# Shifted V copied by two engines, and one batch's keys transposed a stage earlier, in an attention + gated FFN kernel

## The chip, the cores and the metric

The kernel runs on one core of a Trainium2 chip. A core has five engines that run side by side and wait for one another by semaphores: TensorE (PE in the profile, with its weight loads as PEld), VectorE (DVE), ScalarE (ACT), GpSimd (POOL) and SyncE (SP), which here only issues DMA transfers. Each engine works through its own list of instructions in order. The metric is the device time of one execution in microseconds, lower is better.

## The reference

Eight batches of 576 tokens, 8 heads of 64. Attention looks 32 tokens to each side, and 8 global tokens see, and are seen by, everything. Its output goes through a gated feed-forward layer with a gated residual:

```python
scores = scale * np.matmul(q, k.transpose(0, 1, 3, 2))
mask = np.abs(pos[:, None] - pos[None, :]) <= window          # window = 32
mask = mask | is_global[:, None] | is_global[None, :]
scores = np.where(mask, scores, -1000000000.0)
attn = exp(scores - max); attn /= sum(attn); x = np.matmul(attn, v)                 # to [4608, 512]
g = x @ w_gate                                                 # 512 -> 1536
gelu = 0.5 * g * (1.0 + erf(g * inv_sqrt2))
ffn_out = gelu * (x @ w_val) @ w_out                           # 1536 -> 512
out = x + sigmoid(x @ w_res) * ffn_out
```

Inputs and output are float32; the products inside run in bfloat16.

## The kernel before

**Tiling.** The 4608 tokens are cut into 9 chunks of 512. A chunk has 8 windows of 64 queries; a batch has 9 windows, so chunk 1 holds window 8 of batch 0 and windows 0 to 6 of batch 1. A window of 64 queries meets 128 keys. Keys and queries lie transposed in `kt` and `qt`, V lies in rows: `ve` holds blocks of 128 tokens for windows with even i, `vo` the same blocks shifted by 64 tokens for windows with odd i (line 506). `vo` is made from `ve` alone: its lower half of partitions is the upper half of the same block of `ve`, its upper half the lower half of the next block (`shift_v`, lines 102 to 104). All these buffers are in pairs, by the parity of the batch: batch 2 uses the same `kt`, `qt`, `ve`, `vo` as batch 0. `q_st` and `k_st` are single staging buffers, in rows, ahead of the transposing.

**Stages.** The order is written out by hand; a framework adds the semaphore waits. For chunk c, line 702's loop of 12 steps makes the two FFN input products (`g_ps`, `v_ps`, line 550), with ACT's gelu and a DVE product after each. From line 762 follows F(c): for each of four token tiles a gate (`r_ps`, line 568) and three thirds of the output product (`f_ps`, line 593), 16 pieces called `work_f`, between which the attention of chunk c+1 is laid: `scores` (`sc`, exponential on ACT, then the product with the mask on DVE, line 486), `global_rows` (`sn`; its result `vgs` is a DVE product, line 444), `values` (`nd`, from which DVE makes `xtok`), and `turn_x`. A third's end is `prb` on DVE, `ob` on POOL (line 599) and a store issued by SP (line 601). `global_scores(b)` (`sg` and `ss`, lines 415 to 426) for batch b = c+1 is the last thing before F(c) when c > 0; `sg` reads all of `qt`, `ss` all of `kt`. For batch 1 it stands at the start of F(0), and its exponential and the product into `gt` (line 435) follow.

**Loads of batch b >= 2.** `turn_qk(b)` at the start of chunk b-1 (line 696) issues ten DMA transposes on SP, five for q, then five for k. `load_v(b)` on POOL's queue follows (line 697). At step 8 `shift_v(b)` is issued on SP, and `load_qk(b+1)` refills `q_st`, then `k_st`, on POOL's queue, each piece once its transpose has landed.

**Batches 1 and 2 at the start.** They are loaded as float32 and cast by engines. POOL's list in chunk 0, step 5 (lines 720 to 739), is: casts of q and k of batch 1, two casts of `w_res`, five casts of V into `ve[1]`, `shift_v(1)` as two DMAs of POOL's own queue, six casts of `w_out` pieces (14 to 19), three gathers of global rows. The first half of `vo[1]`, as float32, is also where the last V piece of batch 1 is staged. In F(0), lines 772 to 796, batch 2's k and q are loaded (`load_second`), k cast by ACT in one go and q by POOL in three.

Of the kernel before, what the change touches and what calls it, by code (L numbers as in the profile page):

```python
# [23 lines left out]
def kernel(  # L24
# [12 lines left out]
    nc = tc.nc  # L37
# [28 lines left out]
    q_st = const.tile([128, NQT, H * D], BF16, name="q_st", tag="q_st")  # L66
# [35 lines left out]
    def shift_v(b, eng=nc.sync):  # L102
        eng.dma_start(vo[b % 2][0:64, 0:4, :, :], ve[b % 2][64:128, 0:4, :, :])
        eng.dma_start(vo[b % 2][64:128, 0:4, :, :], ve[b % 2][0:64, 1:5, :, :])
# [31 lines left out]
    def cast_piece(n, copy):  # L136
        copy(pieces[n][1], staged(n))
# [56 lines left out]
    def cast_second(what, r0, r1, copy):  # L194
        for r in range(r0, r1):
            n = min(128, S - 128 * r)
            copy({"q": q_st, "k": k_st}[what][0:n, r, :], place2[what][r][0:n, :])
# [208 lines left out]
        copy(dst[:, p, c0:c0 + SM].rearrange("c (s r) -> c s r", r=RPP), ps.rearrange("c r s -> c s r"))  # L406


    def turn_qk(b):
        for src, dst, c0 in ((q_st, qt[b % 2], 0), (k_st, kt[b % 2], 32)):  # L410
            for r in range(NQT):
                n = min(128, S - 128 * r)
                nc.sync.dma_start(dst[:, :, c0 + 128 * r:c0 + 128 * r + n], src[0:n, r, :], transpose=True)

    def global_scores(b):
        sg = psn.tile([128, 2, 512], F32, name="sg", tag="nd")
        for hf in range(2):
            for p in range(NP):
                nc.tensor.matmul(sg[:, hf, 0:288], kgz[b % 2][:, p, :], qt[b % 2][:, p, 288 * hf:288 * hf + 288],  # L419
                                 start=(p == 0), stop=(p == NP - 1))  # L420
        ss = pss.tile([128, 5, 64], F32, name="ss", tag="sc")
        for c in range(5):
            for p in range(NP):
                nc.tensor.matmul(ss[:, c, 16 * p:16 * p + 16], kt[b % 2][:, p, 128 * c:128 * c + 128],
                                 qgz[b % 2][:, p, :], start=True, stop=True)
        return sg, ss

    def global_exp(b, sg, ss):
        rk = 64 * (b % 2)
        rq = 64 - rk  # L430
        nc.scalar.activation(ptg[b % 2][:, :, rq:rq + 64], ss, ACTF.Exp, bias=0.0, scale=SCALE)
        g = gt[b % 2][rk:rk + 64, 64:64 + S]
        nc.scalar.activation(g.rearrange("p (a c) -> p a c", a=2), sg[rk:rk + 64, :, 0:288], ACTF.Exp,
                             bias=0.0, scale=SCALE)
        nc.vector.tensor_tensor(g, g, maskg[rk:rk + 64, :], ALU.mult)
# [89 lines left out]
    def turn_x(c, t):  # L525
        mine = xt[c % 2][:, :, 128 * t:128 * t + 128]
        if c > 1 and t < 3:
            nc.sync.dma_start(mine, xtok[c % 2][:, t, :], transpose=True)
            return
        tx = pss.tile([128, NKT, 128], BF16, name="tx", tag="sc")  # L530
        for kk in range(NKT):
            nc.tensor.transpose(tx[:, kk, :], xtok[c % 2][:, t, 128 * kk:128 * kk + 128], ident)
        (nc.vector.tensor_copy if c or t == 3 else nc.scalar.copy)(mine, tx)  # L533
# [159 lines left out]
    for c in range(NCH):  # L693
        b = c + 1
        if b < B and c:
            turn_qk(b)
            load_v(b)
            if c in (2, 4):
                for what in "kqv":
                    gather(what, c // 2 + 1)  # L700
        held = None
        for j in range(NFF):
            if c or j > 1:
                ffn_in(c, j)
            if c == 0:
                if j == 0:
                    mask_rows(0, NW)
                elif j == 1:
                    mask_rows(NW, NWM)
                    zero_k(1)  # L710
                elif j == 2:
                    zero_gt(1, nc.vector)
                    zero_globals(1)
                    for n in range(1, B // 2):
                        nc.vector.tensor_single_scalar(idx[:, n:n + 1], idx[:, 0:1], float(2 * H * S * n), ALU.add)
                elif j == 3:
                    spread_vg(1, nc.vector)
                elif j == 4:
                    spread_qk(1, compact, 0, {"k": DVE, "q": ACT})
                elif j == 5:  # L720
                    zero_v(1, nc.vector)
                    hot_rows(1)
                    for p in (0, 1, 2, 3, -1):
                        for what in "kq":
                            cast_pair(1, p, what, POOL)
                    load_vraw(1)
                    for n in (14, 15):
                        load_piece(n)
                    for n in (12, 13):
                        cast_piece(n, POOL)  # L730
                    for c5 in range(5):
                        cast_v(1, c5, POOL)
                    shift_v(1, nc.gpsimd)
                    for n in range(16, 20):
                        load_piece(n)
                    for n in range(14, 20):
                        cast_piece(n, POOL)
                    for what in "kqv":
                        gather(what, 1)
                if j > 6:  # L740
                    for what in "kq":
                        turn_pair(1, (0, 1, 2, 3, -1)[j - 7], what)
            elif b < B:
                if c % 2 == 1:
                    n0, n1 = b // 2, b // 2 + 1
                    if j == 8:
                        double_qk(n0, n1)
                    elif j == 9:
                        got = turn_globals(n0, n1)
                        for what in "kq":  # L750
                            DVE(compact[what][:, n0:n1, :], got[what])
                        spread_v(n0, n1)
                if j == 8:
                    shift_v(b)
                    if b + 1 < B:
                        load_qk(b + 1)
                if j == 9:
                    spread_qk(b, compact, (b // 2) * 128, {"k": DVE, "q": DVE})
                    spread_vg(b, nc.vector)
                if j == 11:  # L760
                    held = global_scores(b)
        work_f = [w for t in range(4) for w in ffn_out(c, t)]
        if c == 0:
            global_exp(1, *global_scores(1))
            work_f[0]()
            scores(1, 0)(0, 4)
            work_f[4]()
            work_f[8]()
            mask = scores(1, 1)
            work_f[12]()  # L770
            global_rows(1)
            for what in "kq":
                load_second(what)
            cast_second("k", 0, NQT, ACT)
            work_f[1]()
            values(1, 0)
            mask(0, 2)
            work_f[5]()
            values(1, 1)
            mask(2, 4)  # L780
            work_f[2]()
            turn_x(1, 0)
            work_f[6]()
            values(1, 2)
            turn_x(1, 1)
            work_f[3]()
            cast_second("q", 0, 1, POOL)
            values(1, 3)
            work_f[7]()
            cast_second("q", 1, 3, POOL)  # L790
            turn_x(1, 2)
            work_f[9]()
            work_f[10]()
            turn_x(1, 3)
            work_f[11]()
            cast_second("q", 3, NQT, POOL)
            for n in (13, 14, 15):
                work_f[n]()
            continue
        jobs = {n: [] for n in range(16)}  # L800
        if c + 1 < NCH:
            if held is not None:
                jobs[0].append(lambda: global_exp(b, *held))
                jobs[3].append(lambda: global_rows(b))
            held_mask = {}

            def half(quad):
                held_mask[quad] = scores(c + 1, quad)

            jobs[1] += [lambda: half(0), lambda: held_mask[0](0, 4)]  # L810
            for t in range(4):
                jobs[5 + 2 * t].append(lambda t=t: values(c + 1, t))
                jobs[7 + 2 * t].insert(0, lambda t=t: turn_x(c + 1, t))
            jobs[5].append(lambda: half(1))
            jobs[6].append(lambda: held_mask[1](0, 2))
            jobs[7].append(lambda: held_mask[1](2, 4))
        for n in range(16):
            for w in jobs[n]:
                w()
            work_f[n]()  # L820
# [29 lines left out]
```

## Time and profile before

| | |
|---|---|
| median of 5 runs | 407.12 us (405.8 to 408.34) |
| the profiled execution | 409.42 us, its span 407.7 us |
| TensorE busy | 390.0 us (96%), mean granted clock 0.995 |
| DVE / ACT / POOL busy | 206.0 / 170.9 / 168.5 us |
| SP's DMA queue | 41.88 MB, 45.0% of 16 DMA engines |
| POOL's DMA queue | 10.37 MB, 44.9% of 16 DMA engines |
| HBM read / written | 39.19 / 9.44 MB |

The span runs from the first to the last recorded instruction; the profiled execution's own time is 1.7 us longer. In the profile a row names the engine, the line of the kernel, the operation and `out<-in` by tile names. A bracket gives the idle time of the engine before the row and what ended it. The chain is followed back from the last instruction, at each step to what released it. TensorE's granted clock is given as a share of full speed.

### The profile page before, as it was taken

Reading aid. Unit: us, or ns where it says so; the run is one execution under the profiler, and the core shown is the slowest. Engines: PE = TensorE matmul, PEld = TensorE weight load, DVE = VectorE, ACT = ScalarE, POOL = GpSimd, SP = SyncE. Lnnn points to the kernel's source line nnn. Section 1 sums busy time; section 2 is a strip of 40 time slices with the busy share of each in tenths; the row PEclk is TensorE's granted clock in tenths of the full one; section 3 lists DMA queues with packets and bytes.
Section 4 is the critical chain, followed back from the end, with each engine's and each line's share of the span. In section 5 each row is a group of like instructions: output and inputs, shape, how many; then the busy total and the mean of one; then the engine's idle time right before and its main releaser. Section 6 shows DMA issues by size and latency. Waiting matters only on the chain.

```text
span 407.7 us, 8114 instructions
## 1 busy us (share of the span) xinstructions
PE 390.0 (96%) x3176; PEld 208.5 (51%) x3176; DVE 206.0 (51%) x430; ACT 170.9 (42%) x282; POOL 168.5 (41%) x206
## 2 busy tenths in 40 slices
PE   4899998997999999999999999999999999999995
PEld 2674555443654465446544654456445644554443
DVE  6668656344554554465544553566336534463422
ACT  6664572433523462336323633352435343633320
POOL 8788766746128712562276325521600220021012
PEclk9999999998999999999999999999999999999999
DMA  8999999599929993999399938993992210031002
GB/s 245 255 383 343 232 304 212 145 142 172 91 79 113 188 111 84 95 165 121 84 123 148 136 90 109 164 123 85 87 147 55 79 64 2 0 92 54 1 26 79
DMA packets 152151, 53.30 MB, mean 131 GB/s; under 512 B 136432, under 2 KB 141424, under 8 KB 152112
## 3 DMA queue, kind: packets, MB, share of 16 engines
q1 hardware_dynamic: 76000, 41.88, 45.0%
q0 software_dynamic: 75552, 10.37, 44.9%
q8 instruction: 25, 0.41, 0.5%
q10 hardware_dynamic: 560, 0.52, 0.4%
q14 instruction: 14, 0.11, 0.1%
HBM read 39.19 MB, written 9.44 MB: 119 GB/s over the span
## 4 chain that ended last, share of the span: by engine, by line
PE 81%; DMA 13%; SPq 2%; POOL 2%; issue 1%; DVE 0%; ACTq 0%; DVEq 0%; POOLq 0%
PE f_ps L593 22%; PE g_ps L550 20%; PE v_ps L550 20%; PE r_ps L568 7%; PE nd L508 4%; DMA extra<-in_moe_w_val_dram 3%; DMA vo<-ve 2%; SPq L177 2%; PE sc L464 2%; PE nd L502 2%; DMA kt<-k_st 2%; DMA wo_t<-in_k_dram 2%; PE sn L441 2%; DMA vraw<-in_v_dram 1%; DMA xtok<-in_v_dram 1%; PE sg L419 1%
## 5 line engine op out<-in xcount | busy, mean ns | idle before, releaser
L557 DVE SCALAR_TENSOR_TENSOR ht<-gsb,v_ps 128x512 bf16<-128x512 bf16 x108 | 74.2, 687 | 94.7 <-PE v_ps L550 89.1
L599 POOL TENSOR_TENSOR ob<-prb,xtok 128x512 f32<-128x512 f32 x35 | 40.4, 1153 | 184.5 <-DVE prb L597 182.6
L556 ACT ACTIVATE gsb<-g_ps 128x512 bf16<-128x512 f32 x108 | 64.5, 597 | 122.7 <-PE g_ps L550 120.4
L550 PE MATMUL g_ps<-xt,wg_t 128*128 128x512 bf16 (+1 forms) x440 | 111.2, 375 | 0.4 <-ACT xt L533 0.3
L550 PE MATMUL v_ps<-xt,wv_t 128*128 128x512 bf16 (+1 forms) x440 | 111.2, 375 | 0.0
L593 PE MATMUL f_ps<-wo_t,ht 128*128 128x512 bf16 x420 | 100.4, 379 | 0.0
L550 PEld LDWEIGHTS <-wv_t 128*128 128x128 bf16 x440 | 43.0, 98 | 50.2
L550 PEld LDWEIGHTS <-wg_t 128*128 128x128 bf16 x440 | 42.6, 98 | 49.1 <-issue 0.4
L593 PEld LDWEIGHTS <-ht 128*128 128x128 bf16 x420 | 37.9, 98 | 37.3
L571 ACT ACTIVATE rsb<-r_ps 128x512 bf16<-128x512 f32 x36 | 21.6, 604 | 75.2 <-PE r_ps L568 75.1
L471 ACT ACTIVATE pt<-sc 128x512 bf16<-128x512 f32 x72 | 37.4, 610 | 4.2 <-PE sc L464 4.2
L597 DVE SCALAR_TENSOR_TENSOR prb<-rsb,f_ps 128x512 f32<-128x512 bf16 x35 | 24.0, 686 | 28.7 <-PE f_ps L593 28.2
L568 PE MATMUL r_ps<-wr_t,xt 128*128 128x512 bf16 x144 | 37.6, 385 | 0.1
L486 DVE TENSOR_TENSOR pt<-pt,maskw 128x512 bf16<-128x512 bf16 x64 | 29.0, 469 | 9.7 <-ACT pt L471 7.8
L91 POOL DMA_DIRECT2D q_st<-in_q_dram x25 | 21.3, 856 | 23.3 <-DMA qt<-q_st 22.9
L99 POOL DMA_DIRECT2D ve<-in_v_dram x30 | 25.5, 864 | 0.0
L522 DVE TENSOR_TENSOR xtok<-nd,rden 128x512 bf16<-128x512 f32 x34 | 23.5, 691 | 1.3
L508 PEld LDWEIGHTS <-pt 128*128 128x128 bf16 x576 | 22.2, 97 | 2.3 <-DMA vo<-ve 1.2
L91 POOL DMA_DIRECT2D k_st<-in_k_dram x25 | 21.1, 866 | 4.5 <-DMA kt<-k_st 4.3
L521 DVE RECIPROCAL rden<-nd 128x8 f32<-128x8 f32 x34 | 7.1, 207 | 31.3 <-PE nd L508 29.8
L508 PE MATMUL nd<-ve,pt 128*128 128x65 bf16 x320 | 22.5, 193 | 0.0
L568 PEld LDWEIGHTS <-xt 128*128 128x128 bf16 x144 | 13.6, 98 | 15.4 <-issue 0.6
(144 smaller groups left out, 319.5 us busy)
## 6 DMA issues: line engine op xcount, KB each, us to landing
out_dram<-ob SPq DMA_DIRECT2D x35, 256.0 KB, 2.0
vo<-ve SPq DMA_DIRECT2D x12, 260.0 KB, 5.3
q_st<-in_q_dram POOLq DMA_DIRECT2D x20, 128.0 KB, 6.2
k_st<-in_k_dram POOLq DMA_DIRECT2D x20, 128.0 KB, 6.9
ve<-in_v_dram POOLq DMA_DIRECT2D x18, 128.0 KB, 8.0
wo_t<-in_k_dram SPq DMA_DIRECT2D x8, 256.0 KB, 4.5
extra<-in_moe_w_gate_dram SPq DMA_DIRECT2D x4, 512.0 KB, 8.9
vraw<-in_q_dram SPq DMA_DIRECT2D x8, 256.0 KB, 7.1
```

Source lines behind the costliest of these rows:

```text
L91: nc.gpsimd.dma_start(dst[0:n, r, :].rearrange("p (h d) -> p h d", d=D), src[b].rearrange("h s d -> s h d")[128 * r:128 * r + n])
L99: nc.gpsimd.dma_start(t[p0:p1, c, :, 0:D], v[b].rearrange("h s d -> s h d")[s0 + p0:s0 + p1])
L471: nc.scalar.activation(mine, sc, ACTF.Exp, bias=0.0, scale=SCALE)
L486: nc.vector.tensor_tensor(m, m, view(maskw, 0, 128, 64 * i0, [[0, 2], [64, 4], [1, 64]]), ALU.mult)
L508: nc.tensor.matmul(nds[h // 4][:, VG * (h % 4):VG * (h % 4) + VG], view(pt, 0, 128, c0, [[1, 128]]), vw, start=False, stop=(h % 4 == 3 and ...
L550: nc.tensor.matmul(held[what][:, c0:c1], w[:, kk, 128 * j:128 * j + 128], x[:, kk, c0:c1], start=(kk == 0), stop=(kk == NKT - 1))
L556: nc.scalar.activation(gsb, held["g"], ACTF.Gelu, bias=0.0, scale=1.0)
L557: nc.vector.scalar_tensor_tensor(ht[:, j, :], gsb, 0.5, held["v"], ALU.mult, ALU.mult)
L568: nc.tensor.matmul(r_ps, xt[c % 2][:, kk, 128 * t:128 * t + 128], wr_t[:, kk, :], start=(kk == 0), stop=(kk == NKT - 1))
L593: nc.tensor.matmul(held["f"], ht[:, j, 128 * t:128 * t + 128], wo_t[:, j, :], start=(j == 0), stop=(j == NFF - 1))
L597: nc.vector.scalar_tensor_tensor(prb, held["r"], 1.0, held["f"], ALU.add, ALU.mult)
L599: nc.gpsimd.tensor_tensor(ob, prb, xtok[c % 2][:, t, :], ALU.add)
```

## The change

Two edits. The two DMAs of `shift_v(1)` are replaced by four copies between partition halves: three on POOL, of which one stands where the DMAs stood and two after the last cast of `w_out`, and one on DVE, after the exponential of the global scores at the start of F(0). The fourth block of `vo[1]` is the one that is copied late. And `turn_qk` takes a list of parts: for batch 2 the keys' five transposes are issued in F(0), after the second token tile's store and after POOL's second part of the q casts; chunk 1 then issues only q's.

```diff
-    def turn_qk(b):
-        for src, dst, c0 in ((q_st, qt[b % 2], 0), (k_st, kt[b % 2], 32)):
+    def turn_qk(b, parts="qk"):
+        for what in parts:
+            src, dst, c0 = (q_st, qt[b % 2], 0) if what == "q" else (k_st, kt[b % 2], 32)
             for r in range(NQT):
                 n = min(128, S - 128 * r)
                 nc.sync.dma_start(dst[:, :, c0 + 128 * r:c0 + 128 * r + n], src[0:n, r, :], transpose=True)
...
         if b < B and c:
-            turn_qk(b)
+            turn_qk(b, "q" if c == 1 else "qk")
             load_v(b)
...
                     for c5 in range(5):
                         cast_v(1, c5, POOL)
-                    shift_v(1, nc.gpsimd)
+                    POOL(vo[1][64:128, 0:3, :, :], ve[1][0:64, 1:4, :, :])
                     for n in range(16, 20):
                         load_piece(n)
                     for n in range(14, 20):
                         cast_piece(n, POOL)
+                    POOL(vo[1][64:128, 3:4, :, :], ve[1][0:64, 4:5, :, :])
+                    POOL(vo[1][0:64, 3:4, :, :], ve[1][64:128, 3:4, :, :])
                     for what in "kqv":
                         gather(what, 1)
...
             global_exp(1, *global_scores(1))
+            DVE(vo[1][0:64, 0:3, :, :], ve[1][64:128, 0:3, :, :])
             work_f[0]()
             scores(1, 0)(0, 4)
...
             work_f[7]()
             cast_second("q", 1, 3, POOL)
+            turn_qk(2, "k")
             turn_x(1, 2)
             work_f[9]()
```

## Prediction

> **What bounds the kernel now.** I began with the page's busy shares, then read the chain that ended last, then the engines' timelines at the two places where that chain leaves TensorE (PE).
>
> ```profile
> PE 390.0 (96%) x3176; PEld 208.5 (51%) x3176; DVE 206.0 (51%) x430; ACT 170.9 (42%) x282; POOL 168.5 (41%) x206
> ...
> PEclk9999999998999999999999999999999999999999
> ```
>
> PE is the bound: busy for 390.0 of 407.7 us. Only work taken from PE, or a gap of PE that is closed, moves the end. The first slices and the drain hold most of the gaps; the edit touches neither. The clock row dips below full in one slice only, the tenth (91.7 to 101.9 us). In the chain (start, length, what) two rows are transfers that the diff touches:
>
> ```profile
> 52.87 9.48 DMA vo<-ve
> ...
> 93.06 7.22 DMA kt<-k_st
> ```
>
> So the end is traced back through both. A chain gives the length of a transfer, not how long PE stood. For that I read PE's timeline (start, duration, what, idle before it):
>
> ```profile
> 61.10 0.40 PE L502 MATMUL nd<-vgs,gt 128*128 128x260 bf16 x2 [0.23 <-DVE xtok L522]
> 62.40 0.20 PE L508 MATMUL nd<-vo,pt 128*128 128x65 bf16 x1 [0.90 <-DMA vo<-ve]
> ...
> 95.46 1.14 PE L419 MATMUL sg<-qt,kgz 128*128 128x288 bf16 x8
> 96.44 0.35 PE L424 MATMUL ss<-qgz,kt 128*128 128x16 bf16 x8
> 97.39 0.60 PE L424 MATMUL ss<-qgz,kt 128*128 128x16 bf16 x8 [0.60 <-DMA kt<-k_st]
> 100.33 0.28 PE L424 MATMUL ss<-qgz,kt 128*128 128x16 bf16 x4 [2.33 <-DMA kt<-k_st]
> 100.46 1.87 PE L568 MATMUL r_ps<-wr_t,xt 128*128 128x512 bf16 x4
> 102.26 1.03 PE L464 MATMUL sc<-qt,kt 64*128 64x64 bf16 x32
> ```
>
> The 9.48 us transfer of the shifted V costs PE 0.90 us, the turning of batch 2's keys 0.60 + 2.33 us. After the second gap PE is also slow: the same r_ps and sc rows take 1.02 and 0.64 us one chunk later (at 143.24 and 144.20), so 0.85 + 0.39 us more are lost. The clock, back at 1.00 from 104, explains it (stretch; PE, PEld, DVE, ACT, POOL busy; granted clock; DMA share; GB/s):
>
> ```profile
> 99.00:100.00 1.00, 0.00 (x0) 0.00 (x0) 0.00 (x0) 0.00 (x0) 0.66 (x1) 0.90 1.71 310
> ...
> 101.00:102.00 1.00, 1.00 (x4) 0.15 (x1) 0.36 (x1) 0.61 (x2) 0.53 (x1) 0.50 1.77 157
> ```
>
> **Keys turned in F(0).** I price the whole stage, from the start of sg to the first g_ps of the next chunk: 121.04 - 95.46 = 25.58 us for chunk 1; 162.80 - 141.76 = 21.04 for chunk 2, 204.46 - 183.63 = 20.83 for chunk 3, where q and k are long in place. The excess is 4.54 to 4.75, I take **4.6 us**. The named pieces (2.93 of waiting, 1.24 of slow clock) make 4.17; the rest lies in the broken-up ss rows.
>
> Here a rule of the Trainium skill would shrink the gain. "TensorE: Matmul & The Clock Gate", section "HAM oscillation — how this bites in real kernels", asks that PE have no idle gap over about 3.4 us. The gaps here are 0.60 and 2.33, each below it, so by the rule the clock costs nothing and closing them is worth 2.93 + 0.35, about 3.3 us. The row shows 0.50 all the same; I go by the row.
>
> Are the keys in time? SP's issues now (start, length):
>
> ```profile
> 73.09 7.81 SPq L601 DMA_DIRECT2D out_dram<-ob  x4
> 81.01 6.67 SPq L413 DMA_TRANSPOSE qt<-q_st  x5
> 87.79 7.21 SPq L413 DMA_TRANSPOSE kt<-k_st  x5
> ```
>
> The step that moves is five DMA transposes. Its sources are ready: ACT's last cast into k_st runs 71.18 to 71.80; batch 0's last readers of this kt buffer, the window in scores(1,0), ran at 52.45. It goes behind the second of the four stores, issued at 73.80 and 0.36 long, so it starts at 74.2, takes about 6.7 and ends near 80.9. Landing follows an issue by about 6 to 8 us (last k: 93.06 to 100.28), so k is there by 88 or 89, 7 us before it is read.
>
> Behind it on SP stand the stores of the third and fourth token tiles (their ob ready at 78.3 and 80.5, now issued near 81 and 81.5; nobody waits for these two before F(1)) and then q's five transposes, which start at 81.7 to 82.1 instead of 81.01: **q is 0.7 to 1.1 us later.** GpSimd (POOL) reloads q_st only after these have landed: its waits ended at 87.39, 90.14 and 92.31, and its fifth load was issued at 94.0, so q's last piece had landed by then. Now 95.1 at the latest, and the second half of sg reads it at 95.46 + 0.5 = 96.0. Cost 0; without that cover, microsecond for microsecond. Batch 3's load, queued on POOL behind the same landings, shifts by 1 us for q; the k half finds its buffer free and runs straight on to about 100.5. The next POOL work, ob at 107.99, comes 4.4 us earlier, near 103.6: still clear. The shift of batch 2's V moves forward on SP with it and waits there for its V load, with nothing urgent behind.
>
> **Second batch's V.** The diff removes two DMA issues of POOL (0.56 + 0.54 us) and a 520 KB transfer. It adds one POOL copy of 64x1560, two of 64x520 and one DVE copy of 64x1560. POOL's 64x1040 copies took 1.12 and 1.16; by elements 1560 costs up to 1.73, and by the slope of its casts (0.61 for 512, 1.04 for 1024 elements: 0.18 + 0.83 ns each) 1.48; I take **1.6**. The 64x520 ones cost 0.61 each, after the last wo_t cast, ahead of the gathers of batch pair 1 (not read before 91) and ob. DVE's 64x1040 copy took 0.72, of which about 0.45 was waiting for a POOL cast; alone 1560 would be some 0.5; the V casts that it must wait for are over at 52.02. Only windows with odd i up to 5 are read in chunk 1, so the late fourth chunk of vo is not missed before the following chunk.
>
> If copies only cost their own time, V is ready near 54.5, the 0.90 us goes and nothing is lost: +0.9. But DVE and POOL are not independent here:
>
> ```profile
> L486 DVE TENSOR_TENSOR pt<-pt,maskw x8: 411/575/1253, 54.0 to 65.0; 128x512 bf16<-128x512 bf16 x8
> ...
> L486 DVE TENSOR_TENSOR pt<-pt,maskw x64: 411/425/1253, 54.0 to 360.6; 128x512 bf16<-128x512 bf16 x64
> ```
>
> The mask product takes 0.41 us (least, median, longest in ns) where POOL is quiet and up to 1.25 in F(0), where the long ones end some 0.3 us after a POOL cast does. That is the rule of "SBUF — State Buffer", section "Who interferes with whom": a DVE instruction with two SBUF inputs, or a copy in a two-port mode, and a GpSimd instruction that reads SBUF exclude each other for the whole instruction. By it they alternate, and the edit puts one more long holder on each side. Working it through: POOL copy 52.07 to 53.7; the gt product (ready at 52.91) to 54.0; cast to 55.05; DVE copy to 55.5; cast to 56.5; mask to 56.8; cast to 57.85; mask to 58.1; cast to 59.15; masks to 59.7, where they ended at 57.43. Behind the masks on DVE stands vgs (L444, 0.69), now done at 58.87, just when PE's nd wants it (58.92): then done at 60.4, PE 1.5 us late. The nd that read vo at 62.40 could have run at 61.35 + 1.5 = 62.85: a loss of 0.45. Later masks meet fewer casts and may return 0.2. So by the row without exclusion +0.9, by the rule -0.45; the rows in F(0) side with the rule, so I take **-0.2**.
>
> **Sum.** 4.6 - 0.2 = 4.4 us. The profiled execution took 409.42 around a span of 407.7 (1.7 outside), so it would become 405.0 with a span of 403.3. The median of the runs, 407.12, lies 2.3 below that execution; the saving is a length of PE standing and carries over: **402.7 us**. Chunks 2 to 7 run on a full PE (42.00 busy in the stretch 121 to 163) and give nothing back.
>
> **Rivals.** (1) The V gain is real: POOL and DVE happen to miss each other, or the wo_t pieces, freed of 520 KB of competing transfer, come at better moments. For it: four of the eight masks in F(0) are not long. 4.6 + 0.9 gives **401.6**. (2) q becomes the late one in part: transposes slowed by the V load beside them land between 96 and 100. Against it: slack of about 1 to 3 us; for it: DMA share already 2.51 at 86 to 89. Half of the gain goes: **404.9**. (3) Slower: q takes k's place. If SP cannot start the keys at 74 but only near 81 (casts of k_st behind their load, or the transposes held up by the q load before them), the stores and then q follow, starting at 88.5; q's last lands near 101.3, and sg's second half and ss (1.0 us) still follow, where today only a fifth of ss does. r_ps starts at 102.3 against 100.46: +1.8, with V +0.2, **409.1**. It decides from a last q landing after about 100. (4) Nothing happens: this needs q's last landing near 100, where (2) and (3) meet.
>
> **How the numbers follow.** The main case has 0.68 and its own range 401.8 to 403.6 (4.54 to 4.75, V from -0.45 to +0.2, 0.3 of run-to-run spread each way). Rival 1 has 0.17, rival 2 with 4 0.09, rival 3 0.06. The range 401.0 to 404.7 takes in rival 1 and the near half of rival 2. Half a per cent, 2.0 us, is about what a measurement of this kernel tells from no change, so faster means under 405.1: 0.68 + 0.17 + 0.05 = 0.90; same 0.04; slower 0.06.
>
> **What would show it.** Right: no kt<-k_st wait before ss near 96, the clock at full there, r_ps 1.5 us after sg, a chunk 1 stage of about 21; k's transposes at 74 on SP, q's near 82. In F(0): no vo wait at the nd rows, but longer gt, copy and mask rows on DVE, and PE standing for vgs just before 60. Wrong: a qt<-q_st wait at sg, SP standing ahead of the key transposes, or the gt and mask rows no longer than now.

## Result and the profile after

The changed kernel takes **404.54 us** (median of 30 runs, 401.93 to 406.77) against 407.55 us (51 runs, 405.3 to 410.72) for the kernel before: a ratio of 0.9925, 95% interval 0.991 to 0.9941. That is 3.0 us saved (2.4 to 3.7). The forecast was 4.4 us saved and 402.7 us.

The page of the profiled execution (span 402.5 us, 404.18 us in all), its busy shares and clock row:

```profile
PE 388.1 (96%) x3176; PEld 208.1 (52%) x3176; DVE 207.2 (51%) x431; ACT 170.7 (42%) x282; POOL 170.1 (42%) x207
...
PEclk9999999999999999999999999999999999999999
```

PE is still the bound. The dip in the tenth slice of the clock row is gone. Behind `turn_qk` a line number of the kernel after is one or more higher than that of the same line before. PE's timeline at the two places where the old chain left PE (start, duration, what, idle before it):

```profile
59.48 0.60 PE L503 MATMUL nd<-vgs,gt 128*128 128x260 bf16 x4 [0.91 <-DVE vgs L445]
...
94.81 1.14 PE L420 MATMUL sg<-qt,kgz 128*128 128x288 bf16 x8
95.78 0.65 PE L425 MATMUL ss<-qgz,kt 128*128 128x16 bf16 x20
96.29 1.02 PE L569 MATMUL r_ps<-wr_t,xt 128*128 128x512 bf16 x4
97.25 0.64 PE L465 MATMUL sc<-qt,kt 64*128 64x64 bf16 x32
```

At 95 us the twenty ss products run in one piece, nobody waits for kt, and r_ps and sc have their full-clock durations of 1.02 and 0.64. In F(0) the wait for the shifted V is gone, and PE waits 0.91 us for vgs instead. DVE's timeline shows why (same columns):

```profile
52.48 1.01 DVE L436 TENSOR_TENSOR gt<-gt,maskg 64x576 bf16<-64x576 bf16 x1 [2.12 <-ACT gt L434]
53.52 1.28 DVE L768 COPY vo<-ve 64x1560 bf16<-64x1560 bf16 x1
54.84 3.86 DVE L487 TENSOR_TENSOR pt<-pt,maskw 128x512 bf16<-128x512 bf16 x4
58.73 0.69 DVE L445 TENSOR_TENSOR vgs<-sn,diag 64x520 bf16<-64x520 f32 x1
```

Behind the new copy the masks end at 58.70 and vgs at 59.42. Where the chain that ended last came back through the 9.48 us transfer of vo, it now goes through these DVE rows:

```profile
53.52 1.28 DVE vo L768
...
54.84 3.86 DVE pt L487 x4
```

SP's issues (start and length, with the waiting inside a group):

```profile
54.41 8.78 SPq L191 DMA_DIRECT2D extra<-in_k_dram  x5
...
69.77 2.21 SPq L602 DMA_DIRECT2D out_dram<-ob  x2
72.58 6.55 SPq L414 DMA_TRANSPOSE kt<-k_st  x5
...
80.28 7.67 SPq L414 DMA_TRANSPOSE qt<-q_st  x5
```

The keys stand between the first two stores and, at 79.22, the other two, as forecast. But all of it comes earlier than the forecast had it: the first store at 69.77 where before it went at 73.09. Nothing in the forecast's main case does that. The experiments trace it.

### The profile page after: what moved, and what is told of

Its sections match the earlier page's. It is cut to its first block, busy times and chain, and to the rows that moved or that the text cites. A ratio compares the mean times of both kernels' runs of the same rounds, so it can differ in the third digit from the quotient of the medians.

```text
span 402.5 us, 8112 instructions
## 1 busy us (share of the span) xinstructions
PE 388.1 (96%) x3176; PEld 208.1 (52%) x3176; DVE 207.2 (51%) x431; ACT 170.7 (42%) x282; POOL 170.1 (42%) x207
## 4 chain that ended last, share of the span: by engine, by line
PE 91%; DVE 2%; DMA 2%; ACT 2%; POOL 1%; issue 1%; POOLq 0%; DVEq 0%
PE g_ps L551 23%; PE v_ps L551 23%; PE f_ps L594 22%; PE r_ps L569 7%; PE nd L509 4%; PE sc L465 2%; PE nd L503 2%; PE sg L420 2%; PE sn L442 2%; DMA qgf<-in_q_dram,idx 2%; DVE pt L487 1%; PE ss L425 1%; PE tx L533 1%; PE sc L454 0%; DMA out_dram<-ob 0%
```

## Experiments

To compare executions I read the same two stages from each profile: **F(0)**, from the first sg of batch 1 (near 48 us) to the first g_ps of chunk 1, and the **chunk 1 stage** of the prediction, from the first sg of batch 2 to the first g_ps of chunk 2. What precedes the two varies by up to 2 us between executions of one kernel and is left out.

### Each part alone

Keys early, with V shifted by DMA as before (against the kernel after):

```
-                    POOL(vo[1][64:128, 0:3, :, :], ve[1][0:64, 1:4, :, :])
+                    shift_v(1, nc.gpsimd)
...
-                    POOL(vo[1][64:128, 3:4, :, :], ve[1][0:64, 4:5, :, :])
-                    POOL(vo[1][0:64, 3:4, :, :], ve[1][64:128, 3:4, :, :])
...
-            DVE(vo[1][0:64, 0:3, :, :], ve[1][64:128, 0:3, :, :])
```

> Only the keys of batch 2 are turned in F(0); V is still shifted by the two transfers. Theory A (a typical execution of the kernel before waits less for the keys than the one whose profile was read, since that execution, at 409.4, was 1.9 us above the median): 2.5 to 3.3 us faster than before, and the profile shows no wait for kt at ss. Theory B (the keys are worth the full 4.6 us and the V part loses 1.5 us): 4.6 us faster. Theory C (q takes over a part of the wait in some executions): 3 us faster with a granted clock that falls below 1.00 in the slow executions.

V copied, with q and k turned together in chunk 1 as before:

```
-            turn_qk(b, "q" if c == 1 else "qk")
+            turn_qk(b)
...
-            turn_qk(2, "k")
```

> Only V is copied by POOL and DVE; q and k of batch 2 are turned together in chunk 1 as before. Theory A: within 0.5 us of before (the transfer's 0.90 us of waiting is exchanged for a wait for vgs of about the same length). Theory B: 1.5 us slower than before. In both the gt product, the copy and the mask products on DVE stay as long as in the profile after (1.0, 1.3 and 3.9 us).

Measured: keys alone **404.19 us, 0.9919 (0.9887 to 0.9951)**, V alone **404.15 us, 0.9917 (0.9886 to 0.9948)**, against 407.2 for the kernel before beside them. Either part alone saves 3.0 us by the medians and 3.3 to 3.4 by the ratios, as much as both together. The gains do not add. Theory A came true for the keys; for V alone both theories missed, for neither had a gain.

PE with the keys alone: the V wait stays, the kt wait is gone:

```profile
61.77 0.20 PE L509 MATMUL nd<-vo,pt 128*128 128x65 bf16 x1 [0.78 <-DMA vo<-ve]
...
94.50 1.38 PE L420 MATMUL sg<-qt,kgz 128*128 128x288 bf16 x8
95.71 0.65 PE L425 MATMUL ss<-qgz,kt 128*128 128x16 bf16 x20
```

PE with V alone: the vgs wait has come, and the kt wait is gone here too, though the keys are turned where they always were:

```profile
59.55 0.60 PE L503 MATMUL nd<-vgs,gt 128*128 128x260 bf16 x4 [1.81 <-DVE vgs L445]
...
95.25 0.65 PE L425 MATMUL ss<-qgz,kt 128*128 128x16 bf16 x20
```

SP with V alone gives the reason: both sets of transposes are about 4 us earlier than before (q 81.01, k 87.79 there), because the k load ahead of them on SP took 7.10 us, not 11.19. The k load before, then SP with V alone:

```profile
54.49 11.19 SPq L191 DMA_DIRECT2D extra<-in_k_dram  x5
```

```profile
55.00 7.10 SPq L191 DMA_DIRECT2D extra<-in_k_dram  x5
...
76.83 6.67 SPq L414 DMA_TRANSPOSE qt<-q_st  x5
83.61 6.46 SPq L414 DMA_TRANSPOSE kt<-k_st  x5
```

That load writes the staging buffer `extra`, from which POOL casts the last pieces of w_out. POOL before, and with V alone (start, duration, what, idle before it):

```profile
62.61 1.04 POOL L137 CAST wo_t<-extra 128x1024 bf16<-128x1024 f32 x1 [3.20 <-DMA extra<-in_moe_w_out_dram]
63.80 1.04 POOL L137 CAST wo_t<-extra 128x1024 bf16<-128x1024 f32 x1 [0.15 <-DMA extra<-in_moe_w_out_dram]
```

```profile
60.32 1.04 POOL L137 CAST wo_t<-extra 128x1024 bf16<-128x1024 f32 x1 [0.64 <-DMA extra<-in_moe_w_out_dram]
```

Before, POOL stands 3.20 us for a w_out piece that is landing beside the 520 KB of the V shift, its last cast ends at 64.84, and SP's k load ends at 65.68. With V alone there is 0.64 of waiting, the last cast ends at 61.36 and SP's load at 62.10. In all fourteen profiles of this document the k load ends 0.4 to 1.0 us after POOL's last w_out cast. So the removed transfer may be what moves SP. This is a coincidence of rows so far; the next run tests it.

### The transfer put back where nobody reads it

V alone again, with the V transfer added as traffic: two DMAs of 260 KB on POOL's queue at the old place, into a spare buffer that is never read.

```
+    spare = const.tile([128, 4 * H * VG], BF16, name="spare", tag="spare").rearrange("p (c h e) -> p c h e", h=H, e=VG)
...
+                    for p0, c0 in ((64, 0), (0, 1)):
+                        nc.gpsimd.dma_start(spare[64 - p0:128 - p0, :, :, :], ve[1][p0:p0 + 64, c0:c0 + 4, :, :])
                     POOL(vo[1][64:128, 0:3, :, :], ve[1][0:64, 1:4, :, :])
```

> V copied as in the kernel with only the V part (which alone had saved 3 us), q and k turned together in chunk 1, but two transfers of the size of the old ones are issued again at their old place on POOL's queue, from ve into a spare buffer that nobody reads. Theory D (the V part saves time because 520 KB less run beside the loads of w_out and of batch 2's k and q, so that the casts, stores and transposes on SP start some 4 us earlier): the wait for kt at ss is back, the q transposes start near 80 to 81 as before and not near 77, and the time is that of the kernel before or up to 0.7 us more. Theory E (it is PE's wait for vo, or the order on POOL, and not the transfer's traffic): still 3 us faster than before.

Measured: **406.9 us, 0.9998 (0.997 to 1.0026)**. The whole gain of the V part is gone, though PE waits for no V transfer in this kernel. The DMA issues (queue, count, KB each, median us to landing):

```profile
extra<-in_moe_w_out_dram SPq DMA_DIRECT2D x4, 512.0 KB, 11.9
...
spare<-ve POOLq DMA_DIRECT2D x2, 260.0 KB, 9.5
```

SP is late again, its k load 9.98 us long, and PE waits for kt again, 2.87 us in three pieces (0.59, 1.67 and 0.61; the longest is shown). SP, then PE:

```profile
54.75 9.98 SPq L192 DMA_DIRECT2D extra<-in_k_dram  x5
...
79.54 6.72 SPq L415 DMA_TRANSPOSE qt<-q_st  x5
```

```profile
96.70 0.26 PE L426 MATMUL ss<-qgz,kt 128*128 128x16 bf16 x4 [1.67 <-DMA kt<-k_st]
```

The loss sits in the chunk 1 stage (the two stages are defined above): 25.81 us against 21.20 with V alone, while F(0) is 24.37 against 25.19. So the saving of the V part is the traffic that it takes off the DMA engines, and it comes by way of the keys. (The two POOL issues that go with it, 1.09 us, are back as well, but POOL's first w_out cast still starts at 53.62, against 53.72 with V alone.) The time of SP's k load sorts all fourteen profiles the same way: 11.19, 10.64, 11.47, 11.35, 12.00 and 9.98 us in the six with the transfer, 7.10 to 8.78 in the eight without. The landing time of the w_out pieces is noisier: in the profiles that give it, 8.3 to 12.1 with the transfer, 6.7 and 9.3 without.

### The kernel before, again: which wait is it?

The kernel before, unchanged: timed once more with a profile, then profiled in two single executions.

> The kernel before, unchanged, to see how the wait for the keys differs from execution to execution. Theory A: the executions spread by some 4 us, those with a lower granted clock are the longer ones, and another profile shows a wait for kt at ss of less than 2.9 us, with little or no slow clock behind it. Theory B: the wait is again about 2.9 us and the clock 0.995 in nearly all of them.

> The kernel before, one profile more, to size the stage from sg of batch 2 to the first g_ps of chunk 2 and F(0) from sg of batch 1 to the first g_ps of chunk 1. The two profiles so far had 25.58 and 24.84 for the first, 25.12 and 24.53 for the second. If the wait for the keys was mis-sized by reading one long execution, the stage is 23 to 25 here; if it was sized rightly, 25.4 or more.

> As the one before it: another execution of the kernel before. Stage 23 to 25 us if the forecast took too long a wait, 25.4 or more if not.

Measured: 407.24 us (12 runs, ratio 1.0001), and 406.68 and 407.87 in the single executions. The chunk 1 stages of these two, 21.14 and 22.06, are shorter than either expectation, and their F(0) is longer. In the execution timed again the kt wait was shorter, as theory A had it, but the clock fell to 0.50 behind it all the same. The profiles differ in a way that the one execution I predicted from could not show. In the table (us), PE begins batch 1 with its first sg; V is there when the wait for vo ends; lead is the time from SP's first q transpose to PE's first sg of batch 2.

| kernel before | PE begins batch 1 | V is there | PE waits for vo | F(0) | lead | PE waits for kt | chunk 1 stage | both stages |
|---|---|---|---|---|---|---|---|---|
| execution of the prediction | 49.51 | 62.40 | 0.90 | 25.12 | 14.45 | 2.93 | 25.58 | 50.70 |
| timed again | 48.77 | 61.45 | 0.70 | 24.53 | 14.00 | 2.08 | 24.84 | 49.37 |
| third execution | 48.36 | 62.35 | 2.00 | 27.94 | 16.49 | 0.15 | 21.14 | 49.08 |
| fourth execution | 47.95 | 62.44 | 2.51 | 28.63 | 15.68 | 1.07 | 22.06 | 50.69 |

V arrives within 1.0 us in all four, and PE at moments 1.6 us apart. In the third and fourth PE came early and stood 2.0 and 2.5 us, and then it ran slowly. The fourth's timeline, and the stretches after the wait (stretch; PE, PEld, DVE, ACT, POOL busy; granted clock; DMA share; GB/s):

```profile
62.44 0.24 PE L508 MATMUL nd<-vo,pt 128*128 128x65 bf16 x1 [2.51 <-DMA vo<-ve]
```

```profile
62.00:64.00 2.00, 1.56 (x18) 1.17 (x19) 0.43 (x2) 0.00 (x0) 1.37 (x2) 0.57 1.18 296
64.00:66.00 2.00, 2.00 (x10) 0.98 (x9) 2.00 (x4) 0.45 (x1) 1.50 (x2) 0.58 1.19 210
```

PE is busy for 1.56 + 2.00 us there; at 0.57 and 0.58 of the clock that is 2.05 us of work, so some 1.5 us are lost on top of the wait. In the third execution the same stretches have 0.66 and 0.50; in the two executions with waits of 0.90 and 0.70 they have 1.00.

So the two waits **trade off**. A long V wait makes F(0) 3 us longer, PE reaches batch 2 later and finds the keys nearly there; a short one brings PE to batch 2 with a lead of 14 us, and it stands for the keys. Each stage moves by over 4 us between executions, their sum by 1.6. Lead and kt wait go together in the other kernels that turn q and k in chunk 1, too: 13.31 and 2.87 with the spare transfer, 17.44 and none with V alone. The lead is not all of it: PE's last wait for kt ended 19.3 us after SP's first q transpose in the execution of the prediction and 17.8 to 18.3 after it in the other three, so the forecast was made from an execution whose keys also landed late.

### The kernel after, again

The kernel after, unchanged: timed once more with a profile, then profiled in two single executions.

> The kernel after, unchanged, on the same chip as the other three: 2.5 to 3.5 us faster than before, and the wait for vgs of about 0.9 us at the first nd of F(0) in its profile again. Theory D: no kt wait, and the order of times is act_both and the one with one ACT copy first, then this one, then the one with the spare transfers, near the kernel before.

> The kernel after, one profile more: the stage from sg to the next g_ps at 20.8 to 21.1 again with no wait for kt, and F(0) near 25 to 26, longer than the 24.5 to 25.1 of the kernel before, because PE stands for vgs 0.9 to 1.5 us. If F(0) is 24.5 or less, the V copies cost nothing there.

> As the one before it: another execution of the kernel after, F(0) 25 to 26 us with a wait for vgs of 0.9 to 1.5 us, the stage after it 20.8 to 21.1.

Measured: **404.99 us, 0.9938 (0.9914 to 0.9963)**, and 402.9 and 405.01 in the single executions. Averages of four profiles each:

| | F(0) | chunk 1 stage | both |
|---|---|---|---|
| before (the four above) | 26.55 | 23.41 | 49.96 |
| after (24.89, 26.00, 24.72, 26.68; 20.82, 20.82, 21.20, 21.19) | 25.57 | 21.01 | 46.58 |
| saved | 0.98 | 2.40 | 3.38 |

The sum agrees with the 3.0 us saved by time. Its split is rough, for before the change each stage moves by over 4 us and there are four profiles.

The chunk 1 stage is steady at 20.8 to 21.2, the value of the later chunks. What varies after the change is F(0), by 2.0 us, and in all four profiles PE waits there for vgs: 0.91, 1.53, 0.87 and 1.92 us. (The two single executions, with 24.72 and 0.87, and 26.68 and 1.92, lie a little outside what was expected.) The vgs wait is not all that varies. A later wait of nd, near 67 us, was 0.47, 1.03, none and 1.32 us in the same order; the last of these:

```profile
67.38 0.40 PE L503 MATMUL nd<-vgs,gt 128*128 128x260 bf16 x2 [1.32 <-DVE xtok L523]
```

The kernel before has it too (0.46, none, 0.69 and 0.98 in the order of its table); what makes it long was not traced. None of these waits cost clock: it reads 1.00 in every 2 us stretch from 56 to 68 us of all four. So the wait that took the place of the V wait is about as long as a short V wait or longer, but the long V waits, which cost the clock as well, are gone.

### The copy moved from VectorE to ScalarE

If the vgs wait is the price of two long holders that exclude each other, taking the copy off DVE should return it.

```
-            DVE(vo[1][0:64, 0:3, :, :], ve[1][64:128, 0:3, :, :])
...
+            ACT(vo[1][0:64, 0:3, :, :], ve[1][64:128, 0:3, :, :])
             cast_second("k", 0, NQT, ACT)
```

> As the kernel after, but the lower half of the shifted V is copied by ACT, behind its last exponential of chunk 1 (near 58.5), in place of DVE ahead of the masks. If exclusion of DVE and POOL makes the masks and vgs late: the four mask products end about 1.2 us earlier, the 0.91 us wait of PE for vgs goes, and the time falls by 0.4 to 0.9 us below the kernel after. If DVE was late for another reason: vgs stays late and nothing changes. ACT's copy takes about 1.5 us and ends near 60, before it is read at 61.4; the casts of k_st behind it start at 62.5 anyway.

Measured: **402.37 us, 0.9881 (0.985 to 0.9912)**, 4.8 us saved. PE, then DVE:

```profile
57.68 0.60 PE L503 MATMUL nd<-vgs,gt 128*128 128x260 bf16 x4 [0.30 <-DVE vgs L445]
```

```profile
51.28 1.76 DVE L436 TENSOR_TENSOR gt<-gt,maskg 64x576 bf16<-64x576 bf16 x1 [2.12 <-ACT gt L434]
53.07 3.83 DVE L487 TENSOR_TENSOR pt<-pt,maskw 128x512 bf16<-128x512 bf16 x4
```

ACT's copy runs from 57.28 and takes 1.49 us, in time for the nd that read it. The vgs wait falls to 0.30, and F(0) is 23.93 us, shorter than in any of the four profiles of the kernel after. The gain over the kernel after, some 1.8 us by the ratios, is more than the 0.4 to 0.9 expected; the one profile shows 0.6 of it in the vgs wait against the 0.91 of the kernel after, and none of the later wait of nd. But gt takes 1.76 us and the four masks 3.83: they still wait for POOL's copy and casts. It is the DVE copy's own place in the row that is saved, not the exclusion. This has the lowest ratio of all kernels here; against the kernel after the intervals of the ratios just touch (0.9912 and 0.991), so its lead is likely, not settled.

The same copy on ACT, with q and k turned together in chunk 1 as before:

```
-            turn_qk(b, "q" if c == 1 else "qk")
+            turn_qk(b)
...
-            turn_qk(2, "k")
```

> As the kernel in which ACT copies the lower half of V (4.8 us faster than before), but with q and k of batch 2 turned together in chunk 1. Theory D (the two edits are substitutes: each alone takes away the wait for kt): the same time as with the early keys, within 0.5 us, and no kt wait at ss. If the early keys are needed beside it: 2 to 4 us slower than with them, with a kt wait.

Measured: 403.7 us, 0.9924 (0.99 to 0.9949). A short wait for kt is back, at a lead of 16.63 us:

```profile
95.55 0.26 PE L425 MATMUL ss<-qgz,kt 128*128 128x16 bf16 x4 [0.27 <-DMA kt<-k_st]
```

The stage is no longer for it: 21.25 us, against 21.28 with the early keys. F(0) is 24.65 against 23.93. By the ratios (0.9881 and 0.9924) the early keys are ahead by some 1.8 us, but the intervals overlap, so neither "the same time" nor "2 to 4 us slower" is settled. That the keys' earlier place is worth something beside this copy is not shown beyond the row's 0.27 us.

Both long copies on ACT, POOL keeping only its two late ones, and the keys early again (against the kernel after):

```
-                    POOL(vo[1][64:128, 0:3, :, :], ve[1][0:64, 1:4, :, :])
...
-            DVE(vo[1][0:64, 0:3, :, :], ve[1][64:128, 0:3, :, :])
...
+            ACT(vo[1][0:64, 0:3, :, :], ve[1][64:128, 0:3, :, :])
+            ACT(vo[1][64:128, 0:3, :, :], ve[1][0:64, 1:4, :, :])
```

> As the kernel in which ACT copies the lower half of V, but ACT copies the upper half of the first three blocks too, right behind; POOL keeps only the two late copies. If exclusion of DVE and POOL is what delayed DVE: the gt product falls back from 1.76 to about 0.46 us, the masks end about 0.9 us earlier, vgs no longer makes PE wait (0.30). Against it ACT's second copy ends near 60.3 where vo is read near 60.1: PE waits there up to 0.4 us. In sum the same as with one ACT copy, within 0.5 us.

Measured: 403.05 us, 0.9902 (0.9879 to 0.9926). DVE's gt, then PE:

```profile
52.45 0.46 DVE L436 TENSOR_TENSOR gt<-gt,maskg 64x576 bf16<-64x576 bf16 x1 [2.12 <-ACT gt L434]
```

```profile
61.49 0.19 PE L509 MATMUL nd<-vo,pt 128*128 128x65 bf16 x1 [0.46 <-DMA extra<-in_k_dram]
```

With no POOL copy, gt takes 0.46 us against 1.01 and 1.76: its length was POOL's copy. The four masks take 3.13. The wait for vgs is gone, and a wait of 0.46 for vo is back. The row puts it down to a DMA, but that nd reads vo, and ACT's second copy ends at 61.44, 0.05 before it: two copies of 1.5 us in a row on ACT are too late for it. One on each of POOL and ACT is the better split by the medians, though the intervals overlap.

## Why the prediction was right or wrong

**The direction and the two mechanisms held.** PE was the bound. For the keys, the kt wait went, the clock stayed at full, and the chunk 1 stage went to the forecast 21. For V, the vo wait went, and DVE's longer row made PE stand for vgs instead.

**That the time fell within the stated range is in part luck.** The measured 404.54 lies outside the main case's own range, 401.8 to 403.6 (whose upper end, by the terms that it names, is 407.12 - (4.54 - 0.45 - 0.3) = 403.3). It lies inside the wider range, which had been drawn out to 404.7 for a late q, and q was not late. Two errors also cancel in half: against the stage averages above, the keys were taken for 2.2 us too much and the V part for 1.2 us too little.

**The step that was mis-sized: "I take 4.6 us" for the keys.** It came from one execution, in which the V wait was short (0.90) and the kt wait long (2.93). Over four profiles of before the stage's excess is 23.41 - 21.01 = **2.4 us**. The keys alone saved 3.3 us by time (2.0 to 4.6), and beside the copied V nothing that can be measured (0.9917 with V alone, 0.9925 with both). The V part's -0.2, which the forecast meant beside the early keys, is not contradicted by the times: 0.9919 with the keys alone and 0.9925 with both is -0.2 us, with some 1.5 us of doubt either way. But its working was not whole. It set copies against one short wait. It left out the traffic (V alone saves 3.4 us, and nothing once the traffic is put back) and the long V waits (F(0) became 0.98 us shorter on average, not longer). Both edits cure the late keys, so either alone gives about 3 us, and so do both.

**Rival 1 named the right thing for the wrong place.** It had the w_out pieces "freed of 520 KB of competing transfer" come at better moments, and priced this inside F(0) at 0.9 on top of the keys. The freed transfer is what the spare-transfer run shows to matter, but through SP: casts free `extra` sooner, k's load ends 2.5 us sooner (63.19 against 65.68), and the transposes follow. That gain is the keys' gain, not one beside it. (Of this path the spare transfer tested its two ends; the steps between are read from the rows.)

**The timings on SP.** The keys started at 72.58, forecast 74.2; q at 80.28, forecast 81.7 to 82.1. Both are early by the shift of the whole chain. With the transfer still there (keys alone) they are 74.67 and 82.52: q 1.5 us later than before, where 0.7 to 1.1 was forecast. The cover was thin there: sg took 1.38 instead of 1.14, about 0.24 us, and the profile shows its weight load waiting for qt. With V copied sg has its 1.14, so rivals 2 and 3, a late q, did not come. The next ob came at 102.58, forecast 103.6.

**Exclusion of DVE and POOL.** Here the rule of the Trainium skill ("SBUF — State Buffer", "Who interferes with whom") was rightly put above the cost of the copies alone: the two engines exclude each other there, and without that the V part would have been +0.9 and the masks no later. POOL's copy took 1.48 us (forecast 1.6), gt 1.01 and the DVE copy 1.28. Gt took 0.46 where POOL had neither copy nor cast beside it, and the DVE copy 0.68 in the spare-transfer run, in which it came just ahead of POOL's. The masks ended at 58.70 (forecast 59.7), and PE stood 0.87 to 1.92 us for vgs in four profiles (forecast 1.5 late).

**The clock.** The choice of the row over the page's 3.4 us ("TensorE: Matmul & The Clock Gate", "HAM oscillation — how this bites in real kernels") held: in the new profiles of before the clock fell after gaps of 2.00 and 2.51 us, where the page's limit would have it cost nothing and some 1.5 us of work were lost. In the one timed again it fell to 0.50 at 100 to 102 us after gaps of 1.40 and 0.68, and in the spare-transfer run after 0.59, 1.67 and 0.61. After gaps of 0.70 and 0.90 (vo), and of 1.81 and 1.92 (vgs), it stayed at 1.00. So the V wait costs clock too when it is long, which the forecast did not price. No run varied the gap alone: 1.92 and 2.00 lie close together, and the length need not be all that decides.

What stays open: why chunk 0, ahead of both stages, brings PE to batch 1 up to 1.6 us sooner in one execution than in another. No run here changed anything ahead of that point. Nor was the V transfer tried with PE's arrival held fixed; that a long V wait and a short kt wait go together, and that the clock loss comes from the length of the wait, rests on four profiles.

## What to carry to other kernels

Before pricing a wait from a profile, ask what else would change its length: two waits one behind the other can trade off, as here, and one execution shows one split of them, so price their sum from several. A removed transfer is worth what it takes from the DMA engines as well as the wait that it ended: follow which buffers come free sooner and what is queued behind them, and do not add two edits that cure the same lateness. When a copy must leave the DMA engines and VectorE is busy beside GpSimd, try the engine that stands idle at that point, here ScalarE (the lowest ratio of all, 0.9881, though its lead over the kernel after is not settled).

## What was unexpected of the hardware

- PE's granted clock fell to about half after one long gap of 2.00 or 2.51 us (0.50 to 0.66 in the 2 us stretches that follow), and after 1.40 + 0.68 us with a few small products between them. Gaps of 1.53, 1.81 and 1.92 us, for vgs, left it at 1.00.
- 520 KB moved within the core's own memory (SBUF) on POOL's queue held up loads on SP's queue enough to shift q's transposes by 2 to 5 us (79.54 and later where both are turned in chunk 1, against 76.83 and 77.12), and the V part's saving vanished with it (ratio 0.9917 to 0.9998), though nobody waited for those bytes.
- A partition-shifted copy of 64x1560 bf16 took 1.48 to 1.68 us on POOL, 1.49 on ACT, and on DVE 0.68 when it ran just ahead of POOL's copy and 1.28 to 1.74 beside or behind it; the two DMAs of 260 KB that they replace took 7.5 to 9.7 us each from issue to landing.
